# Selective attention and spectral mixing: q and k in runs of 18 tokens, two batches per transfer, on two partition halves

## The chip, the cores and the metric

The kernel runs on one core of a Trainium2 chip. The metric is the device time of one execution in microseconds (us). An execution reads all its inputs from HBM and writes its result there.

## What is computed

Two stages follow each other. The first is causal attention over 8 batches, 8 heads, 576 tokens and 64 dimensions per head, with a bias made of cumulative sums of a selector `s`. The second takes the first 64 Fourier modes along the tokens, mixes their channels with one complex 512x512 matrix per mode, goes back, and adds a projection with a ReLU.

```python
scores = scale * np.matmul(q, k.transpose(0, 1, 3, 2))
cum = np.cumsum(np.maximum(s, 0.0), axis=-1)
bias = -(cum[:, :, :, None] - cum[:, :, None, :])
scores = np.where(causal, -1000000000.0, scores + np.minimum(bias, 0.0))
attn = softmax(scores)
x = np.matmul(attn, v)                      # heads side by side: (8, 576, 512)

X = np.fft.rfft(x, axis=1)[:, :64]
Y[:, :64] = einsum('bmd,mde->bme', X, w_r + 1j * w_i)   # 64 complex 512x512 matrices
u = x + np.fft.irfft(Y, n=576, axis=1)
out = u + np.maximum(u @ w_ch, 0.0)
```

The inputs are float32. The matrices `w_r` and `w_i` are 134 MB of them, and q, k and v 9.4 MB each.

## The kernel before

The attention works on pairs of heads. There are N = 32 steps: step n takes batch n % 8 and the head pair n // 8 (the variable `g`). Each step needs q, k and v of its pair of heads. The weights of the spectral stage are loaded all the time beside this, in tiles of 4 modes x 128 input channels. Once the 8 steps of a head pair `g` are transformed (after step 7, 15, 23 and 31), the products of its 128 channels (`modes`, L444) use the weights, one set of 8 modes per step or so.

**Loads.** All large loads are issued by GpSimd (POOL), in program order, and are cast from float32 to bf16 (or fp16) on the way. `loads_qkv` (L147) makes the list for one step: q, k, and v in two parts. `loads_w` (L200) makes the list of weight transfers, two of 256 KB for each tile, one for each half of the partitions. `load` (L222) mixes the lists it is given evenly and issues them at L226. In step n it mixes the q, k and v of step n + 3 (LA = 3) with the weights that should be on chip by then (`on_chip`). A load into a buffer waits until the last reader of the buffer is done. q and k have LA + 1 = 4 buffers each, v has 5, and the weights have two rings of 11 and 6 tiles beside 8 places in tensors that are not in use yet.

**How q and k lie.** A step's two heads lie on the 128 partitions, 64 partitions to a head, and each partition has R = 9 consecutive tokens of 64 values. A run is therefore 9 x 64 x 4 = 2304 bytes read and 1152 bytes written, and each of q and k is one transfer of 128 runs (144 KB written).

**Transposes.** The scores need the 64 dimensions on the partitions. `transposes(n, which)` (L323) turns q (which = 0) or k (which = 1) with 18 small TensorE transposes (L333) into one PSUM tile, `tr_ps`, of which there is only one buffer. Two copies (L336) take it to SBUF: the first head on partitions 0 to 63 of `qtA` or `ktA`, the second head on partitions 64 to 127 of `qtB` or `ktB`. Row 64 of `qtA` and row 0 of `qtB` hold the negated cumulative sums (`cum_rows`, L315), and the same rows of `ktA` and `ktB` hold ones, so that the matmul adds the bias. The rest of the lower half of `qtB` and `ktB` is zero. The first head's matmuls thus contract over 65 rows, the second head's over 128 (L374).

**The order of one step** (L549 to L573) is written out by hand: loads for step n + 3; `cum_rows(n + 1)`; scores of the first head; `av` (attention times v) of the step before, second head; transposes of q for step n + 1; scores of the second head; transposes of k for step n + 1; the Fourier transform of step n - 1 (`fft`); `av` of the first head; then the modes that are due. TensorE executes this list in order. So a transpose that waits for q or k holds up all that stands behind it on TensorE.

After the steps, the remaining weights of the last group are loaded and multiplied, the result is projected, and 9.4 MB are written out.

Of the kernel before, what the change touches and what calls it, by code (L numbers as in the profile page):

```python
# [11 lines left out]
BF16 = mybir.dt.bfloat16  # L12
# [6 lines left out]
def kernel(  # L19
# [11 lines left out]
    nc = tc.nc  # L31
    B, H, S, D = q.shape
    NM = moe_w_r.shape[0]
    DM = H * D
    P = 128
    NT = (S + P - 1) // P
    tails = [min(P, S - T * P) for T in range(NT)]
    NL = tails[NT - 1]
# [4 lines left out]
    NCH = D + 1  # L43
    N = NG * B
# [4 lines left out]
    WA, WB = 11, 6  # L49
    LA = 3  # L50
    NF = NT - 1
    R = S // (P // 2)
    RP = P // 2
    W = 2 * P
    NWN = S // W
    NK = 2 * NWN
# [1 line left out]
    HP = P // 2  # L58
# [52 lines left out]

    at = ExitStack()
    ap_ = at.enter_context(tc.tile_pool(name="attn", bufs=1))
    qkpool = at.enter_context(tc.tile_pool(name="qk_sb", bufs=LA + 1))
    cumt_sb = ap_.tile([P, NK + 1, NPAIR], FP32, name="cumt_sb")
    cumt4 = ap_.tile([P, NPAIR // 2], FP32, name="cumt4")
    ncum_sb = ap_.tile([NPAIR, S], BF16, name="ncum_sb")
    NQ = 2
    qtA = [ap_.tile([NCH, S], BF16, name=f"qtA{i}") for i in range(NQ)]
    qtB = [ap_.tile([P, S], BF16, name=f"qtB{i}") for i in range(NQ)]  # L120
    ktA = [ap_.tile([NCH, S], BF16, name=f"ktA{i}") for i in range(NQ)]
    ktB = [ap_.tile([P, S], BF16, name=f"ktB{i}") for i in range(NQ)]
    NV = LA + 2
    VW = 66

# [18 lines left out]

    loaded = {}

    def loads_qkv(n):  # L147

        if n >= N:
            return []  # L150
        g, b = divmod(n, B)
        hs = slice(2 * g, 2 * g + 2)
        q2 = qkpool.tile([P, R + 1, D], BF16, name="q2", tag="q2")[:, :R, :]
        k2 = qkpool.tile([P, R + 1, D], BF16, name="k2", tag="k2")[:, :R, :]
        loaded[n] = (q2, k2)
        todo = [
            (dst, src[b, hs].rearrange("h (p r) d -> (h p) r d", r=R))
            for src, dst in ((q, q2), (k, k2))
        ]
        todo += [  # L160
            (
                v2[n % NV][:, : 2 * NWN * W].rearrange("p (w h c) -> p w h c", w=NWN, h=2)[:, :, h, P:],
                v[b, 2 * g + h, : NF * P, :].rearrange("(w p r) d -> p w (r d)", p=P, r=2),
            )
            for h in range(2)
        ]
        return todo

    def loads_tails(g):

        if g >= NG:
            return []
        return [
            (
                v4[g % 2][NL * h : NL * h + NL, :, :D],
                v[:, 2 * g + h, NF * P :, :].rearrange("b t d -> t b d"),
            )
            for h in range(2)
        ]
# [42 lines left out]
    def load(*lists):  # L222

        todo = [((i + 0.5) / len(l), x) for l in lists for i, x in enumerate(l)]
        for _, (dst, src) in sorted(todo, key=lambda t: t[0]):
            nc.gpsimd.dma_start(out=dst, in_=src)  # L226
# [8 lines left out]
    W0 = 3  # L235
    on_chip = []
# [15 lines left out]
    nc.sync.dma_start(out=s_sb, in_=s.rearrange("b h t -> (b h) t"))  # L252
    nc.sync.dma_start(out=ident32, in_=d_ident32)
    nc.sync.dma_start(out=negm32, in_=d_negm)
    first, second, tails0 = loads_qkv(0), loads_qkv(1), loads_tails(0)
    load(first[:2])
    load(loads_w(W0), first[2:] + tails0 + second)
    nc.sync.dma_start(out=Ff_sb, in_=d_Ff.rearrange("(T p) c -> p T c", p=P))
    nc.sync.dma_start(out=ident16h, in_=d_ident16h)
    nc.sync.dma_start(out=G_sb, in_=d_G)  # L260
# [2 lines left out]
    nc.vector.memset(zero, 0.0)  # L263
    nc.scalar.activation(out=zero, in_=zero, func=ACTF.Exp)
    for i in range(NQ):
        nc.vector.memset(qtB[i][0:64, :], 0.0)
        nc.vector.memset(ktB[i][0:64, :], 0.0)
        nc.vector.memset(ktB[i][0:1, :], 1.0)
        nc.vector.memset(ktA[i][D : D + 1, :], 1.0)
    for i in range(NV):  # L270
        for c in (P - 1, W):
            nc.vector.memset(
# [42 lines left out]
    def cum_rows(n):  # L315
        if n >= N:
            return
        g, b = divmod(n, B)
        p0 = b * H + 2 * g
        nc.sync.dma_start(out=qtA[n % NQ][D : D + 1, :], in_=ncum_sb[p0 : p0 + 1, :])  # L320
        nc.sync.dma_start(out=qtB[n % NQ][0:1, :], in_=ncum_sb[p0 + 1 : p0 + 2, :])

    def transposes(n, which):  # L323
        if n >= N:
            return
        src = loaded[n][which]
        dA, dB = ((qtA, qtB), (ktA, ktB))[which]
        g, b = divmod(n, B)
        ps = trpool.tile([P, R, RP], BF16, name="tr_ps", tag="tr")
        for r in range(R):  # L330
            for h in range(2):
                rows = slice(D * h, D * h + D)
                nc.tensor.transpose(ps[rows, r, :], src[rows, r, :], ident16[rows, rows])  # L333
        for dst, rows in ((dA, slice(0, D)), (dB, slice(D, P))):
            copy = (nc.vector.tensor_copy, nc.scalar.copy)[which == 1 and dst is dB]
            copy(  # L336
                out=dst[n % NQ][rows, :].rearrange("d (p r) -> d p r", r=R),
                in_=ps[rows].rearrange("d r p -> d p r"),
            )

    def scores4(n, ps):

        g, b = divmod(n, B)
        i0 = NF * P
        nc.tensor.matmul(
            ps, ident16, negm[:, 2 * W :], start=False, stop=False, skip_group_check=True
        )
        for h, (kt, qt) in enumerate(((ktA, qtA), (ktB, qtB))):
            nc.tensor.matmul(  # L349
                ps[NL * h : NL * h + NL, :], kt[n % NQ][:, i0:], qt[n % NQ][:, i0:],  # L350
                start=False, stop=True, skip_group_check=True,
            )
        nc.scalar.activation(  # L353
            out=p4[n % 2][:, :NL], in_=ps, func=ACTF.Exp,
            bias=cumt4[:, b * (H // 2) + g : b * (H // 2) + g + 1], scale=0.125,
        )

    def scores(n, h):
        g, b = divmod(n, B)
        pidx = b * H + 2 * g + h  # L360
        qt = (qtA, qtB)[h][n % NQ]
        pt = p_sb[(2 * n + h) % NP_]
        keys = (ktA, ktB)[h][n % NQ][:, : NF * P].rearrange("c (w p r) -> c w r p", p=P, r=2)
        for r in range(2):
            ps = scpool.tile([P, 1024], FP32, name="sc_ps", tag="sc")

            for w in range(NWN):
                nc.tensor.matmul(  # L368
                    ps[:, bass.ds(w * S, W)], ident16, negm[:, bass.ts(r, W)],
                    start=True, stop=False, skip_group_check=True,  # L370
                )
            for w, i0, i1 in ((0, 0, 512), (0, 512, S), (1, W, S)):
                c0 = w * S + i0 - w * W
                nc.tensor.matmul(  # L374
                    ps[:, c0 : c0 + i1 - i0], keys[:, w, r, :], qt[:, i0:i1],
                    start=False, stop=True, skip_group_check=True,
                )
            if h == 1 and r == 0:
                scores4(n, ps[:, 2 * S - W : 2 * S - W + NL])
            for w in range(NWN):  # L380
                x = 2 * w + r
                nc.scalar.activation(  # L382
                    out=pt[:, poff[x] : poff[x] + S - w * W], in_=ps[:, w * S : (w + 1) * S - w * W],
                    func=ACTF.Exp, bias=cumt_sb[:, x, pidx : pidx + 1], scale=0.125,
                )
# [155 lines left out]
    with tc.tile_pool(name="sc_psum", bufs=2, space=PSUM) as scpool, \  # L541
            tc.tile_pool(name="tr_psum", bufs=1, space=PSUM) as trpool, \
            tc.tile_pool(name="av_psum", bufs=1, space=PSUM) as avpool:
        cum_rows(0)
        transposes(0, 0)
        transposes(0, 1)
        load(loads_qkv(2))
        pad_p()
        for n in range(N):  # L549
            if n in (0, 2):  # L550
                nc.vector.memset(xs_flat[n // 2].bitcast(FP32), 0.0)
            tails_due = loads_tails(n // B + 1)[n % B - 3 : n % B - 2] if 2 < n % B < 5 else []
            load(loads_qkv(n + LA) + tails_due, loads_w(on_chip[n]))
            cum_rows(n + 1)
            scores(n, 0)
            av(n - 1, 1)
            transposes(n + 1, 0)
            scores(n, 1)
            i = first_pairs[n - N + len(first_pairs)] if n >= N - len(first_pairs) else None
            if i is not None:  # L560
                first_transposed(i, 0)
            transposes(n + 1, 1)
            fft(n - 1)
            av(n, 0)
            if i is not None:
                first_product(i, 0)
                first_transposed(i, 1)
            for c in mode_steps.get(n, []):
                modes(c // NCK, c % NCK)
            if i is not None:  # L570
                first_product(i, 1)
            if n == N // 2:
                nc.gpsimd.dma_start(out=wch_sb, in_=moe_w_ch.rearrange("(dt p) e -> p dt e", p=P))  # L573
        av(N - 1, 1)
        fft(N - 1)
# [354 lines left out]
```

## Time and profile before

| | |
|---|---|
| time, median of 3 runs | 448.7 us (448.08 to 450.4) |
| span of the profiled execution | 445.7 us |
| written by DMA | 93.30 MB, mean 209 GB/s |
| read from HBM | 163.51 MB, 388 GB/s over the span with what is written |
| packets of queue q0 (issued by POOL) | 67984, 81.29 MB |
| q or k transfer, issue to landing | 7.1 us (median of 32 each) |
| weight transfer, issue to landing | 8.0 us |

The page divides the span into 40 slices and gives the busy share of each engine in tenths. Bytes are counted as written: a load that casts float32 to bf16 reads twice what it writes. A group line gives the source line, the engine, the operation, the tile written and the tile read, and how many there are; then the total busy time and the mean of one in ns; then the idle time ahead of them and what ended it. A line of a list of waits names who waited, for what, the sum in us, how often, and the longest. Line numbers are those of the kernel before.

### The profile page before, as it was taken

Reading aid. Unit: us, or ns where it says so; the run is one execution under the profiler, and the core shown is the slowest. Engines: PE = TensorE matmul, PEld = TensorE weight load, DVE = VectorE, ACT = ScalarE, POOL = GpSimd, SP = SyncE. Lnnn points to the kernel's source line nnn. Section 1 sums busy time; section 2 is a strip of 40 time slices with the busy share of each in tenths; the row PEclk is TensorE's granted clock in tenths of the full one; section 3 lists DMA queues with packets and bytes.
Section 4 is the critical chain, followed back from the end, with each engine's and each line's share of the span. In section 5 each row is a group of like instructions: output and inputs, shape, how many; then the busy total and the mean of one; then the engine's idle time right before and its main releaser. Section 6 shows DMA issues by size and latency. Waiting matters only on the chain.

```text
span 445.7 us, 11492 instructions
## 1 busy us (share of the span) xinstructions
PE 355.5 (80%) x4729; PEld 222.3 (50%) x4729; DVE 251.0 (56%) x576; ACT 218.7 (49%) x387; POOL 259.8 (58%) x405
## 2 busy tenths in 40 slices
PE   1889987997575989967767887888897896769994
PEld 1557665665344655644445354556664455433341
DVE  7777764675243656643445445556654454441885
ACT  1586766366242654744426254556550434220593
POOL 7766665755566675556675655566544544430393
PEclk9999997999575889975869796999997999988999
DMA  9999999999999999999999999999999999996598
GB/s 183 201 202 205 204 203 205 204 207 206 208 207 202 196 193 202 208 207 207 205 202 206 206 207 207 207 204 203 207 210 210 209 210 210 209 217 121 173 353 345
DMA packets 77251, 93.30 MB, mean 209 GB/s; under 512 B 30144, under 2 KB 39872, under 8 KB 77200
## 3 DMA queue, kind: packets, MB, share of 16 engines
q0 software_dynamic: 67984, 81.29, 105.5%
q1 hardware_dynamic: 9216, 11.29, 7.8%
q8 instruction: 37, 0.61, 0.5%
q14 instruction: 14, 0.11, 0.1%
HBM read 163.51 MB, written 9.44 MB: 388 GB/s over the span
## 4 chain that ended last, share of the span: by engine, by line
DMA 62%; PE 21%; POOL 5%; issue 5%; DVE 4%; POOLq 1%; ACT 0%; SPq 0%; DVEq 0%
DMA w_sb<-in_moe_w_i_dram 26%; DMA w_sb<-in_moe_w_r_dram 15%; DMA q<-in_q_dram 10%; DMA k<-in_k_dram 9%; PE yp L452 4%; PE sc_ps L374 3%; POOL r_w L766 3%; PE z_ps L624 2%; PE av_ps L403 2%; PE tr_ps L333 2%; PE sc_ps L368 2%; PE ft_ps L429 2%; POOL w_sb L226 2%; DMA qtA<-ncum_sb 1%; DMA xs<-c_negm 1%
## 5 line engine op out<-in xcount | busy, mean ns | idle before, releaser
L382 ACT ACTIVATE p_sb<-sc_ps,cumt_sb 128x576 f16<-128x576 f32 (+1 forms) x256 | 142.0, 636 | 58.7 <-PE sc_ps L374 58.2
L226 POOL DMA_DIRECT2D w_sb<-in_moe_w_r_dram x120 | 71.6, 597 | 61.1 <-DMA w_sb<-in_moe_w_r_dram 18.5
L226 POOL DMA_DIRECT2D w_sb<-in_moe_w_i_dram x120 | 71.3, 595 | 49.4 <-DMA w_sb<-in_moe_w_i_dram 17.3
L226 POOL DMA_DIRECT2D v<-in_v_dram x72 | 51.8, 719 | 22.4 <-DMA w_sb<-in_moe_w_r_dram 7.1
L368 PE MATMUL sc_ps<-negm,ident 128*128 128x256 bf16 x256 | 55.6, 303 | 0.4
L452 PE MATMUL yp<-w_sb,xs 128*32 128x512 bf16 (+1 forms) x480 | 42.5, 431 | 12.3 <-DMA w_sb<-in_moe_w_i_dram 5.6
L403 PE MATMUL av_ps<-v,p_sb 128*128 128x65 f16 x1024 | 45.2, 199 | 0.0
L333 PE MATMUL tr_ps<-ident,q 64*64 64x64 bf16 x576 | 16.6, 205 | 33.3 <-DMA q<-in_q_dram 33.3
L336 DVE COPY ktA<-tr_ps 64x576 bf16<-64x576 bf16 x32 | 24.0, 750 | 33.8 <-PE tr_ps L333 33.8
L403 PEld LDWEIGHTS <-p_sb 128*128 128x128 f16 x1024 | 39.4, 101 | 5.4 <-DVE x_all L413 2.3
L374 PE MATMUL sc_ps<-qtB,ktB 128*128 128x512 bf16 (+2 forms) x192 | 41.4, 330 | 0.0
L336 DVE COPY qtA<-tr_ps 64x576 bf16<-64x576 bf16 x32 | 23.8, 742 | 29.1 <-PE tr_ps L333 28.9
L374 PE MATMUL sc_ps<-qtA,ktA 65*128 65x512 bf16 (+2 forms) x192 | 38.6, 313 | 0.6 <-DMA qtA<-ncum_sb 0.6
L439 DVE CAST xs<-ft_ps 64x128 bf16<-64x128 f32 x128 | 31.4, 284 | 8.3 <-PE ft_ps L429 7.7
L353 ACT ACTIVATE p<-sc_ps,cumt 128x64 f16<-128x64 f32 x32 | 10.1, 314 | 52.7 <-PE sc_ps L349 52.7
L408 DVE TENSOR_REDUCE den<-av_ps 128x5 f32<-128x10 f32 x64 | 10.9, 170 | 43.6 <-PE av_ps L403 42.8
L429 PE MATMUL ft_ps<-Ff_sb,x_all 128*64 128x96 f16 (+1 forms) x640 | 33.2, 224 | 1.0 <-DVE x_all L413 1.0
L452 PEld LDWEIGHTS <-xs 128*32 128x32 bf16 (+1 forms) x512 | 19.8, 145 | 28.4 <-issue 16.6
L413 DVE TENSOR_TENSOR x_all<-av_ps,rcp 128x320 f16<-128x320 f32 x64 | 31.4, 491 | 2.2
L333 PE MATMUL tr_ps<-ident,k 64*64 64x64 bf16 x576 | 16.8, 206 | 19.0 <-DVE qtB L336 10.0
L336 ACT COPY ktB<-tr_ps 64x576 bf16<-64x576 bf16 x32 | 20.3, 634 | 22.3 <-DVE ktA L336 21.4
L333 PEld LDWEIGHTS <-q 64*64 64x64 bf16 x576 | 12.9, 118 | 35.8 <-DMA q<-in_q_dram 34.7
(119 smaller groups left out, 558.1 us busy)
## 6 DMA issues: line engine op xcount, KB each, us to landing
w_sb<-in_moe_w_r_dram POOLq DMA_DIRECT2D x120, 256.0 KB, 8.0
w_sb<-in_moe_w_i_dram POOLq DMA_DIRECT2D x117, 256.0 KB, 8.1
out_dram<-r_w SPq DMA_DIRECT2D x14, 512.0 KB, 3.0
q<-in_q_dram POOLq DMA_DIRECT2D x32, 144.0 KB, 7.1
k<-in_k_dram POOLq DMA_DIRECT2D x32, 144.0 KB, 7.1
v<-in_v_dram POOLq DMA_DIRECT2D x72, 64.0 KB, 6.9
x_all<-in_moe_w_i_dram POOLq DMA_DIRECT2D x6, 256.0 KB, 6.8
out_dram<-r_w SPq DMA_DIRECT2D x6, 256.0 KB, 3.2
```

Source lines behind the costliest of these rows:

```text
L226: nc.gpsimd.dma_start(out=dst, in_=src)
L333: nc.tensor.transpose(ps[rows, r, :], src[rows, r, :], ident16[rows, rows])
L336: copy(out=dst[n % NQ][rows, :].rearrange("d (p r) -> d p r", r=R), in_=ps[rows].rearrange("d r p -> d p r"),)
L368: nc.tensor.matmul(ps[:, bass.ds(w * S, W)], ident16, negm[:, bass.ts(r, W)], start=True, stop=False, skip_group_check=True,)
L374: nc.tensor.matmul(ps[:, c0 : c0 + i1 - i0], keys[:, w, r, :], qt[:, i0:i1], start=False, stop=True, skip_group_check=True,)
L382: nc.scalar.activation(out=pt[:, poff[x] : poff[x] + S - w * W], in_=ps[:, w * S : (w + 1) * S - w * W], func=ACTF.Exp, bias=cumt_sb[:, x, ...
L403: nc.tensor.matmul(ps[:, I, r : r + NCH], lhsT, rhs, start=(i == 0), stop=(i == len(todo) - 1), skip_group_check=True,)
L413: nc.vector.tensor_tensor(out=x_all[:, g, b, :, D * h : D * h + D], in0=ps[:, :, 1 : NCH], in1=rcp.unsqueeze(2).to_broadcast([P, NT, D]), ...
L429: nc.tensor.matmul(ps[HP * h : HP * h + HP, q_, :], x_all[:nT, g, b, T, q_::2], Ff_sb[:nT, T, 3 * HM * h : 3 * HM * (h + 1)], start=(T == ...
L439: nc.vector.tensor_copy(out=xs[g % 2][rows, :, k, h, :, b, :], in_=ps[rows, :, k * HM : (k + 2) * HM].rearrange("p q (r m) -> p q r m", r=2),)
L452: nc.tensor.matmul(ps[32 * cg : 32 * cg + 32, :], cols[k0:, q_, 1 - ri, :, c * MC // 2 + cg], wt[(g, c, ri, cg // 2)][k0:, 2 * (cg % 2) + ...
L766: nc.gpsimd.tensor_tensor(out=rs[i], in0=rs[i], in1=z1s[i], op=ALU.add)
```

## The change

q and k are laid out anew. 32 partitions now hold a head, and each partition holds R = 18 consecutive tokens. A run is 4608 bytes read and 2304 bytes written. q has partitions 0 to 63 and k partitions 64 to 127 of one tile, and the tile has room for two batches. One transfer of q and one of k load both batches; the first two batches are loaded one by one, so that the first can start early. Two such tiles take the place of four buffers each of q and k, and pairs are asked for only in steps of odd n. The transposes of a step are again two calls, but each now takes 9 of the 18 tokens of every partition, of q and of k together. The destinations are `qt` and `kt`, with both heads side by side along the free dimension and 65 rows for either head. The zeros and the 128-row contraction of the second head go away.

The purpose is to move the same bytes of q and k in longer runs and in fewer transfers.

```diff
-    R = S // (P // 2)
-    RP = P // 2
+    RP = P // 4
+    R = S // RP
+    RH = R // 2
...
-    qkpool = at.enter_context(tc.tile_pool(name="qk_sb", bufs=LA + 1))
+    qkpool = at.enter_context(tc.tile_pool(name="qk_sb", bufs=2))
...
-    qtA = [ap_.tile([NCH, S], BF16, name=f"qtA{i}") for i in range(NQ)]
-    qtB = [ap_.tile([P, S], BF16, name=f"qtB{i}") for i in range(NQ)]
-    ktA = [ap_.tile([NCH, S], BF16, name=f"ktA{i}") for i in range(NQ)]
-    ktB = [ap_.tile([P, S], BF16, name=f"ktB{i}") for i in range(NQ)]
+    qt = [ap_.tile([NCH, 2, S], BF16, name=f"qt{i}") for i in range(NQ)]
+    kt = [ap_.tile([NCH, 2, S], BF16, name=f"kt{i}") for i in range(NQ)]
...
-        todo = [
-            (dst, src[b, hs].rearrange("h (p r) d -> (h p) r d", r=R))
-            for src, dst in ((q, q2), (k, k2))
+        t = loaded[n] = loaded[n + 1] = qkpool.tile([P, 2, R * D], BF16, name="qk2", tag="qk2")
+        return [
+            (
+                t[HP * i : HP * i + HP, x0:x1],
+                src[b + x0 : b + x1, hs].rearrange("b h (p r) d -> (h p) b (r d)", r=R),
+            )
+            for x0, x1 in ([(0, 2)] if n else [(0, 1), (1, 2)])
+            for i, src in enumerate((q, k))
         ]
...
-        nc.vector.memset(qtB[i][0:64, :], 0.0)
-        nc.vector.memset(ktB[i][0:64, :], 0.0)
-        nc.vector.memset(ktB[i][0:1, :], 1.0)
-        nc.vector.memset(ktA[i][D : D + 1, :], 1.0)
+        nc.vector.memset(kt[i][D : D + 1], 1.0)
...
-    def transposes(n, which):
+    def transposes(n, half):
...
-        ps = trpool.tile([P, R, RP], BF16, name="tr_ps", tag="tr")
-        for r in range(R):
-            for h in range(2):
-                rows = slice(D * h, D * h + D)
+        src = loaded[n][:, n % 2, :].rearrange("p (r d) -> p r d", d=D)[:, half * RH : half * RH + RH]
+        ps = trpool.tile([P, RH, 2 * RP], BF16, name="tr_ps", tag="tr")
+        for r in range(RH):
+            for i in range(2):
+                rows = slice(HP * i, HP * i + HP)
                 nc.tensor.transpose(ps[rows, r, :], src[rows, r, :], ident16[rows, rows])
-        for dst, rows in ((dA, slice(0, D)), (dB, slice(D, P))):
-            copy = (nc.vector.tensor_copy, nc.scalar.copy)[which == 1 and dst is dB]
+        for i, dst in enumerate((qt, kt)):
+            copy = (nc.vector.tensor_copy, nc.scalar.copy)[half * i]
+            to = dst[n % NQ][:D].rearrange("d h (p r) -> d h p r", r=R)
             copy(
-                out=dst[n % NQ][rows, :].rearrange("d (p r) -> d p r", r=R),
-                in_=ps[rows].rearrange("d r p -> d p r"),
+                out=to[:, :, :, half * RH : half * RH + RH],
+                in_=ps[HP * i : HP * i + HP].rearrange("d r (h p) -> d h p r", h=2),
             )
...
-            load(loads_qkv(n + LA) + tails_due, loads_w(on_chip[n]))
+            load((loads_qk(n + LA) if n % 2 else []) + loads_v(n + LA) + tails_due, loads_w(on_chip[n]))
```

More of the change, by code (lines that the diff above doesn't have):

```diff
@@ L145, with loads_qk @@
     loaded = {}
-    def loads_qkv(n):
+    def loads_qk(n):
         if n >= N:
@@ L152, in loads_qkv, with loads_v @@
         hs = slice(2 * g, 2 * g + 2)
-        q2 = qkpool.tile([P, R + 1, D], BF16, name="q2", tag="q2")[:, :R, :]
-        k2 = qkpool.tile([P, R + 1, D], BF16, name="k2", tag="k2")[:, :R, :]
-        loaded[n] = (q2, k2)
-        todo = [
-            (dst, src[b, hs].rearrange("h (p r) d -> (h p) r d", r=R))
-            for src, dst in ((q, q2), (k, k2))
-        ]
-        todo += [
+        t = loaded[n] = loaded[n + 1] = qkpool.tile([P, 2, R * D], BF16, name="qk2", tag="qk2")
[6 more added lines that the diff above has]
+            for i, src in enumerate((q, k))
+        ]
+    def loads_v(n):
+        if n >= N:
+            return []
+        g, b = divmod(n, B)
+        return [
             (
@@ L166, in loads_qkv @@
         ]
-        return todo
     def loads_tails(g):
@@ L254 @@
     nc.sync.dma_start(out=negm32, in_=d_negm)
-    first, second, tails0 = loads_qkv(0), loads_qkv(1), loads_tails(0)
+    first = loads_qk(0)
     load(first[:2])
-    load(loads_w(W0), first[2:] + tails0 + second)
+    load(loads_w(W0), loads_v(0) + loads_tails(0) + first[2:] + loads_v(1))
     nc.sync.dma_start(out=Ff_sb, in_=d_Ff.rearrange("(T p) c -> p T c", p=P))
@@ L319, in cum_rows @@
         p0 = b * H + 2 * g
-        nc.sync.dma_start(out=qtA[n % NQ][D : D + 1, :], in_=ncum_sb[p0 : p0 + 1, :])
-        nc.sync.dma_start(out=qtB[n % NQ][0:1, :], in_=ncum_sb[p0 + 1 : p0 + 2, :])
-    def transposes(n, which):
+        for h in range(2):
+            nc.sync.dma_start(out=qt[n % NQ][D : D + 1, h, :], in_=ncum_sb[p0 + h : p0 + h + 1, :])
+    def transposes(n, half):
         if n >= N:
             return
-        src = loaded[n][which]
-        dA, dB = ((qtA, qtB), (ktA, ktB))[which]
-        g, b = divmod(n, B)
-        ps = trpool.tile([P, R, RP], BF16, name="tr_ps", tag="tr")
-        for r in range(R):
-            for h in range(2):
-                rows = slice(D * h, D * h + D)
+        src = loaded[n][:, n % 2, :].rearrange("p (r d) -> p r d", d=D)[:, half * RH : half * RH + RH]
[3 more added lines that the diff above has]
+                rows = slice(HP * i, HP * i + HP)
                 nc.tensor.transpose(ps[rows, r, :], src[rows, r, :], ident16[rows, rows])
-        for dst, rows in ((dA, slice(0, D)), (dB, slice(D, P))):
-            copy = (nc.vector.tensor_copy, nc.scalar.copy)[which == 1 and dst is dB]
+        for i, dst in enumerate((qt, kt)):
+            copy = (nc.vector.tensor_copy, nc.scalar.copy)[half * i]
+            to = dst[n % NQ][:D].rearrange("d h (p r) -> d h p r", r=R)
             copy(
-                out=dst[n % NQ][rows, :].rearrange("d (p r) -> d p r", r=R),
-                in_=ps[rows].rearrange("d r p -> d p r"),
+                out=to[:, :, :, half * RH : half * RH + RH],
+                in_=ps[HP * i : HP * i + HP].rearrange("d r (h p) -> d h p r", h=2),
             )
@@ L347, in scores4 @@
         )
-        for h, (kt, qt) in enumerate(((ktA, qtA), (ktB, qtB))):
+        for h in range(2):
             nc.tensor.matmul(
-                ps[NL * h : NL * h + NL, :], kt[n % NQ][:, i0:], qt[n % NQ][:, i0:],
+                ps[NL * h : NL * h + NL, :], kt[n % NQ][:, h, i0:], qt[n % NQ][:, h, i0:],
                 start=False, stop=True, skip_group_check=True,
@@ L360, in scores @@
         pidx = b * H + 2 * g + h
-        qt = (qtA, qtB)[h][n % NQ]
+        qh = qt[n % NQ][:, h, :]
         pt = p_sb[(2 * n + h) % NP_]
-        keys = (ktA, ktB)[h][n % NQ][:, : NF * P].rearrange("c (w p r) -> c w r p", p=P, r=2)
+        keys = kt[n % NQ][:, h, : NF * P].rearrange("c (w p r) -> c w r p", p=P, r=2)
         for r in range(2):
@@ L374, in scores @@
                 nc.tensor.matmul(
-                    ps[:, c0 : c0 + i1 - i0], keys[:, w, r, :], qt[:, i0:i1],
+                    ps[:, c0 : c0 + i1 - i0], keys[:, w, r, :], qh[:, i0:i1],
                     start=False, stop=True, skip_group_check=True,
@@ L546 @@
         transposes(0, 1)
-        load(loads_qkv(2))
+        load(loads_qk(2) + loads_v(2))
         pad_p()
```

## The prediction

> **What bounds the kernel now.** I read the page's engine shares and its slices first, then the chain of waits, then the waits of TensorE, and last the answer by windows.
>
> ```profile
> PE 355.5 (80%) x4729; PEld 222.3 (50%) x4729; DVE 251.0 (56%) x576; ACT 218.7 (49%) x387; POOL 259.8 (58%) x405
> DMA  9999999999999999999999999999999999996598
> q0 software_dynamic: 67984, 81.29, 105.5%
> DMA 62%; PE 21%; POOL 5%; issue 5%; DVE 4%; POOLq 1%; ACT 0%; SPq 0%; DVEq 0%
> ```
>
> No compute engine is above 80%, while the 16 DMA engines stand at 9 tenths in the first 36 slices. The chain that ended last is 62% DMA. The 105.5% of queue q0 is over 100% because packets overlap on an engine.
>
> ```profile
> PE tr_ps L333 <- DMA q<-in_q_dram: 33.3, 12, 6.4
> PE tr_ps L333 <- DVE qtB L336: 10.0, 15, 2.0
> ...
> PE tr_ps L333 <- DMA k<-in_k_dram: 8.4, 8, 2.0
> PE yp L452 <- DMA w_sb<-in_moe_w_i_dram: 5.6, 4, 2.1
> ```
>
> These are TensorE's longest repeated waits (us, times, longest). It waits for q, k and weights to arrive: it runs ahead of the stream and is held by it.
>
> ```profile
> 20.00:320.00 300.00, 245.35 (x3816) 164.22 (x3813) 168.40 (x420) 164.60 (x312) 189.39 (x308) 0.86 1.20 205
> 330.00:390.00 60.00, 49.25 (x455) 28.42 (x452) 30.30 (x55) 19.05 (x27) 27.91 (x48) 0.94 1.12 210
> ```
>
> The last two columns are the DMA share and GB/s written. The attention stage moves 205 GB/s, the stage with weights alone 210. The small difference is what smaller packets cost; it is the whole subject of the change.
>
> Is the stream ever starved? POOL issues 393 transfers, and in the trace 337 of these go out while exactly 7 earlier ones are still under way. The least after 30 us is 4. In quarter-microseconds of the packet records, the number of packets in flight falls below 16 only twice, near 163 us, for 0.06 us of work in all. So to 409 us (landing of the last weight) the time is the sum of the packets' costs, and from there to 445.7 a tail of 36.5 us follows (last modes, results), in which nothing that the change touches runs.
>
> [...] I price it from the trace. With a fixed cost f per data packet and b per byte written, 16 engines x time = packets x f + bytes x b. From 20 to 320 us there are 50,126 data packets and 61.33 MB in 4.80 million engine-ns; from 330 to 390 us 6,109 packets and 12.58 MB in 0.96 million. Solved: **b = 0.0734 ns/B, f = 6.0 ns**. Each written byte is a bf16 half of 2 read bytes, so b is 27.3 GB/s of reads per engine[...]. [...] The weights here are already loaded into halves of 64 partitions and still run at 210 GB/s[...]. [...]
>
> **The change part by part.**
>
> 1. *Longer runs.* q and k are 64 transfers of 128 packets of 1152 B (8,192 in all). After: 4,096 packets of 2304 B, the same bytes. The saving is one fixed cost per merged pair, and its size is the disputed number. Low end: f = 6.0 ns, 4,096 x 6.0 / 16 = 1.5 us. High end: a single 1152 B packet lasts 107 ns and a 2048 B packet 173 ns in the records; that line has an intercept of 22 ns, but packets overlap (share 1.20), so little of the 22 is throughput; taken in full it gives 4,096 x 22 / 16 = 5.6 us. Between: if each size has its own price, a fit over stretches of 2.5 us gives 92 +- 5 ns for 1152 B (stretches of 5 us: 102 +- 7), against 6.0 + 84.6 = 90.6 on the line. A 2304 B packet should cost 6.0 + 169.1 = 175. I take the finer fit: 2 x 92 - 175 = 9 ns, x 4,096 / 16 = **2.3 us**. No run here shows a cast packet of 2304 B.
>
> 2. *Fewer transfers.* 64 become 34 (the first two batches keep single loads). Each ends in 16 completion packets; at f each, 30 x 16 x 6 / 16 = **0.2 us** at most. POOL spends 30 x 0.575 = 17 us less on issuing, but POOL waits for a free place among the transfers anyway; the stream hides it.
>
> 3. *Order of loads and waits.* A pair goes out in the load list of an odd n, where before one batch went. Its tile was last used by the pair before the last, so POOL waits for the second transposes of batch n. In the trace POOL issued q(n+3) 3.1 us (n = 1) and from n = 3 on 6 to 26 us after those transposes had begun. So this wait is over before it is asked; behind it in POOL's queue are v and weights, which would otherwise be held. Nothing.
>
> 4. *Transposes in two halves.* The first half now needs q **and** k. In the trace k landed after TensorE had started on q at nearly every even n from 8 to 28, by 0.2 to 4.3 us (21 us in 9 batches). TensorE will stop longer there; behind it stand the second scores, fft, av and modes. At odd n it has its data a whole iteration early and doesn't stop. TensorE needs 6.8 us per batch where it does not wait (batches 3 to 7), about 8.3 with one set of modes, and the stream gives it 10 to 15. It catches up within the pair. The modes' buffers come free up to some 4 us later every second iteration; 5 transfers in flight x 1.25 us (256 KB at 210 GB/s) cover 6 us. I book nothing, and keep this as the main risk.
>
> 5. *Evictions.* Three DVE copies (739, 760, 750 ns) and one ACT copy (634) per batch, 64x576 each, before and after. The destination now has runs of 9 with steps of 18 elements. Bounds: nothing, to twice as long (2.2 us per batch on DVE). DVE is at 56%; either is under the stream's 10 us per batch. Nothing.
>
> 6. *Second head with 65 rows instead of 128.* The 512-column matmul took 443 ns with 128 rows and 419 with 65; at most 64 x 24 + 64 x 20 + 64 x 9 ns = 3.4 us of TensorE, beside the stream. Memsets (eight become two) run before the constants land at 6.3 us. The two rows of sums per batch stay 64 small transfers. Nothing.
>
> Sum: 2.3 + 0.2 = 2.5 us off the stream; the tail moves with it. 448.7 - 2.4 = **446.3 us** (I leave 0.1 us for dips).
>
> **The rivals.**
>
> *A: the full 22 ns count.* For it: the clean intercept of the durations. Against: the two stages, solved together, leave 6 ns. 5.6 us, and 30 x 22 ns = 0.7 us for completions: 442.4 us.
>
> *B: the longer stop for k starves the stream, and it ends slower.* For it: twelve times TensorE began within 0.05 us of q's landing, so each stop is real, and the weights' buffers are released behind it; at 162, 178 and 245 us only 5 transfers were in flight. Against: the cover of 6 us. If at each of ten even batches 1 us to 0.5 us gets through, that is 5 to 10 us, less the 2.5: some 453 us.
>
> *C: a read of 4608 B is cut in two[...], or is dearer.* The longest cast read here is 4096 B, so nothing in the trace decides it. The packets stay 8,192: 448.5 us.
>
> **How the numbers follow.** Forecast 0.60, A 0.12, B 0.16, C 0.12. The threshold of 0.5% is 446.5 us, almost on the forecast: its case splits, half faster (0.30), half same. Faster: 0.30 + A 0.12 + 0.01 = 0.43. Same: 0.29 + C 0.12 = 0.41. Slower: 0.16. The range runs from 443.2 (most of the way to A) to 449.6 (C, the spread of the runs before, and the mild end of B).
>
> **What would show it.** Packets of 2304 B, 4,096 of them on q0, each about 192 ns long. Queue q0's packets down by some 4,600. The last weight landing near 406.8 instead of 409.2 us, the tail still 36 to 37 us. TensorE waits for k rather than q at L333, in every second batch only. Wrong would be: DMA slices below 9 before 400 us, or POOL idle on TensorE with fewer than 4 transfers in flight (B); packets of 1152 B or of uneven sizes (C); a stream shorter by 5 us (A).

## The result and the profile after

The changed kernel takes **461.48 us** (median of 4 runs, 458.63 to 462.29), the kernel before 448.93 us in the same session. The ratio is 1.0265, 95% interval 1.0212 to 1.0317: slower by 12.6 us, where 2.4 us less was forecast.

The same rows of the page as before, now of the changed kernel: engine shares, the DMA slices, bytes moved in each slice, queue q0, and the shares of the chain.

```profile
PE 382.1 (83%) x4729; PEld 238.6 (52%) x4729; DVE 249.6 (54%) x570; ACT 222.2 (48%) x387; POOL 242.8 (53%) x375
...
DMA  9999999993999999999999999999999999998498
GB/s 180 201 207 206 203 187 204 145 162 50 203 205 210 203 206 207 188 208 207 208 203 203 207 208 202 208 206 207 206 210 209 211 209 210 209 214 157 147 351 347
...
q0 software_dynamic: 63408, 81.29, 101.4%
...
PE 48%; DMA 35%; DVE 6%; POOL 3%; issue 3%; ACT 2%; POOLq 1%; SPq 0%; DVEq 0%; ACTq 0%
```

The packets did what was asked: q0 has 4,576 fewer, 4,096 of data and 480 that end 30 transfers (5,808 packets of 4 B for 363 transfers, 6,288 for 393 before: 16 for each). But the chain, 62% DMA before, is now 48% TensorE and 35% DMA. In slices 8 to 10 of GB/s, each 11.5 us long (80 to 115 us), the stream falls to 145, 162 and 50. It has a hole, and the packet records size it: the engines idle there make up 13.1 us of the whole stream, against 0.06 us before. What follows is shifted, not slowed: 20 MB of queue q0 are written at 120.7 us instead of 105.1, and 80 MB at 414.9 instead of 400.2. The last weight lands at 423.7 us instead of 409.2, and the tail is 36.2 us against 36.5.

Who made the hole? First the lines of POOL's waits (who waited, for what; us in total, times, longest), one of the kernel before and two of the changed one, then POOL's own instructions around the longest one (start, us, what, idle before and its releaser).

```profile
POOL w_sb L226 <- PE yp L452: 6.4, 9, 1.1
```

```profile
POOL w_sb L232 <- PE yp L454: 25.3, 7, 14.4
...
POOL qk L232 <- PE tr_ps L334: 13.3, 3, 7.0
```

```profile
94.37 1.21 POOL L232 DMA_DIRECT2D w_sb<-in_moe_w_r_dram  x2
110.01 0.59 POOL L232 DMA_DIRECT2D w_sb<-in_moe_w_r_dram  x1 [14.44 <-PE yp L454]
```

POOL stood still for 14.4 us because a weight buffer was not free: its reader, the first modes (`yp`), had not run. The transfers already in flight lasted until 102.1 us, so when POOL went on at 110.0 none was left. So TensorE was late. How late it was shows in the view by windows of 30 us; the columns are busy time of PE, PEld, DVE, ACT, POOL, then PEclk, DMA share and GB/s. Before:

```profile
20.00:50.00 30.00, 26.82 (x479) 19.26 (x476) 22.46 (x57) 23.41 (x45) 20.86 (x34) 1.00 1.21 205
50.00:80.00 30.00, 25.76 (x441) 18.26 (x441) 18.52 (x49) 20.55 (x40) 19.96 (x33) 0.89 1.24 204
80.00:110.00 30.00, 27.34 (x466) 18.68 (x463) 20.08 (x53) 17.68 (x34) 18.42 (x31) 1.00 1.19 206
```

After:

```profile
20.00:50.00 30.00, 30.00 (x326) 19.60 (x324) 15.40 (x37) 17.41 (x33) 18.03 (x29) 1.00 1.20 205
50.00:80.00 30.00, 30.00 (x339) 20.05 (x338) 14.57 (x39) 16.25 (x31) 15.10 (x24) 1.00 1.20 197
80.00:110.00 30.00, 30.00 (x333) 18.20 (x335) 13.68 (x36) 13.52 (x25) 10.05 (x16) 1.00 0.73 121
```

TensorE is shown as busy for all of 90 us and yet executes 326 matmuls in the first window where it executed 479. The profile models the ends of matmuls, but their starts say the same: from 20 to 110 us no two are more than 0.6 us apart. TensorE is not waiting; each matmul is longer. One group shows it. The timeline of TensorE: first before, then after, 18 transposes and the 20 matmuls of the Fourier transform.

```profile
46.53 0.47 PE L333 MATMUL tr_ps<-ident,k 64*64 64x64 bf16 x18 [0.54 <-DMA w_sb<-in_moe_w_i_dram]
46.94 0.98 PE L429 MATMUL ft_ps<-Ff_sb,x_all 128*64 128x96 f16 x20
```

```profile
60.30 0.69 PE L334 MATMUL tr_ps<-ident,qk 64*64 64x64 bf16 x18
60.91 1.43 PE L431 MATMUL ft_ps<-Ff_sb,x_all 128*64 128x96 f16 x20
```

Neither group was changed in its work, and both take about 1.46 times as long. The column PEclk says 1.00, but it has no record there: the trace's first clock record of the changed kernel is "full speed" at 111.0 us, and what lies ahead of a first record is shown as full. In the kernel before, the first such record is at 18.4 us. A step takes 10.1 us instead of 6.8 (the transposes of L334 begin at 60.30, 70.38 and 80.47 us), and the first modes start at 103.8 us instead of 80.3.

### The profile page after: what moved, and what is told of

It is laid out like the page before. It is cut to its first block, busy times and chain, and to the rows that moved or that the text cites. A ratio compares the mean times of both kernels' runs of the same rounds, so it can differ in the third digit from the quotient of the medians.

```text
span 459.9 us, 11427 instructions
## 1 busy us (share of the span) xinstructions
PE 382.1 (83%) x4729; PEld 238.6 (52%) x4729; DVE 249.6 (54%) x570; ACT 222.2 (48%) x387; POOL 242.8 (53%) x375
## 4 chain that ended last, share of the span: by engine, by line
PE 48%; DMA 35%; DVE 6%; POOL 3%; issue 3%; ACT 2%; POOLq 1%; SPq 0%; DVEq 0%; ACTq 0%
DMA w_sb<-in_moe_w_i_dram 12%; DMA w_sb<-in_moe_w_r_dram 11%; DMA qk<-in_k_dram 10%; PE sc_ps L376 9%; PE av_ps L405 8%; PE sc_ps L370 6%; PE yp L454 5%; PE ft_ps L431 5%; PE tr_ps L334 5%; PE z_ps L626 3%; POOL r_w L768 3%; PE z_ps L537 1%; DVE kt L338 1%; DVE qt L338 1%; PE xt_ps L616 1%
## 5 line engine op out<-in xcount | busy, mean ns | idle before, releaser
L232 POOL DMA_DIRECT2D w_sb<-in_moe_w_i_dram x120 | 71.3, 597 | 61.2 <-DMA w_sb<-in_moe_w_i_dram 18.2
L376 PE MATMUL sc_ps<-qt,kt 65*128 65x512 bf16 (+2 forms) x384 | 90.2, 352 | 1.2 <-ACT kt L338 1.1
L338 DVE COPY qt<-tr_ps 64x576 bf16<-64x576 bf16 x64 | 47.8, 747 | 65.9 <-PE tr_ps L334 65.9
L334 PE MATMUL tr_ps<-ident,qk 64*64 64x64 bf16 x1152 | 38.2, 217 | 42.1 <-DMA qk<-in_k_dram 19.9
L376 PEld LDWEIGHTS <-kt 65*128 65x128 bf16 x384 | 45.2, 118 | 33.2 <-issue 13.8
L334 PEld LDWEIGHTS <-qk 64*64 64x64 bf16 x1152 | 29.6, 128 | 53.0 <-DMA qk<-in_k_dram 20.6
L405 PE MATMUL av_ps<-v,p_sb 128*128 128x65 f16 x1024 | 52.2, 213 | 0.0
L405 PEld LDWEIGHTS <-p_sb 128*128 128x128 f16 x1024 | 46.5, 110 | 4.7 <-DVE x_all L415 0.5
L338 ACT COPY kt<-tr_ps 64x576 bf16<-64x576 bf16 x32 | 22.9, 716 | 16.4 <-DVE qt L338 15.9
L431 PEld LDWEIGHTS <-x_all 128*64 128x64 f16 (+1 forms) x640 | 25.3, 126 | 10.6 <-DVE x_all L415 1.1
L370 PEld LDWEIGHTS <-ident 128*128 128x128 bf16 x256 | 19.4, 105 | 14.3 <-PE yp L454 5.1
```

Source lines behind the costliest of these rows:

```text
L338: copy(out=to[:, :, :, half * RH : half * RH + RH], in_=ps[HP * i : HP * i + HP].rearrange("d r (h p) -> d h p r", h=2),)
L370: nc.tensor.matmul(ps[:, bass.ds(w * S, W)], ident16, negm[:, bass.ts(r, W)], start=True, stop=False, skip_group_check=True,)
L376: nc.tensor.matmul(ps[:, c0 : c0 + i1 - i0], keys[:, w, r, :], qh[:, i0:i1], start=False, stop=True, skip_group_check=True,)
L405: nc.tensor.matmul(ps[:, I, r : r + NCH], lhsT, rhs, start=(i == 0), stop=(i == len(todo) - 1), skip_group_check=True,)
L431: nc.tensor.matmul(ps[HP * h : HP * h + HP, q_, :], x_all[:nT, g, b, T, q_::2], Ff_sb[:nT, T, 3 * HM * h : 3 * HM * (h + 1)], start=(T == ...
```

## The experiments

**Theory R**: the second head's 128-row matmuls had brought TensorE to its full clock. With 65 rows it stays at half speed until the modes, falls behind, gives buffers back late, and the stream starves. **Theory O**, the prediction's rival B widened: the new order (pairs, two tiles, a half transpose that needs q and k at once) makes the holes.

**128 rows for the second head again.** All else stays as changed.

```diff
+    KR = (NCH, 128)
+    qt = [ap_.tile([P, 2, S], BF16, name=f"qt{i}") for i in range(NQ)]   # kt alike
...
+        nc.vector.memset(kt[i][D:, 1, :], 0.0)   # qt alike
...
-        qh = qt[n % NQ][:, h, :]
+        qh = qt[n % NQ][: KR[h], h, :]   # keys and scores4 alike
```

> The changed kernel, with one part undone: the second head's matmuls contract over 128 rows again (rows 65 to 127 of its qt and kt are zero). Loads, pairs, two tiles and half transposes stay. Theory R (rows: with 65 rows TensorE's clock is granted in full only at 111 us, so that it falls behind and the stream starves for 13 us): full clock near 18 to 20 us, a step of 6.8 us before step 8, no hole in the stream, 446 to 447 us. Theory O (order: the pair's tile wait and the first half's need of q and k together make the holes): holes of POOL near 60, 80 and 95 us stay, 459 to 462 us.

Measured: 447.44 us (20 runs), ratio to before 0.9979, interval 0.9968 to 0.9990. The first full-clock record is at 23.2 us (half again from 36.9, for 6.8 us). Its slices have no hole:

```profile
DMA  9999999999999999999999999999999999996598
GB/s 176 202 206 205 203 207 204 207 203 208 207 209 203 206 204 179 207 206 208 207 202 206 208 208 207 208 207 203 200 210 210 211 211 208 209 218 132 176 352 340
```

TensorE does wait for k in this kernel, as the prediction had feared; here is that line of its waits:

```profile
PE tr_ps L337 <- DMA qk<-in_k_dram: 28.4, 8, 4.9
```

28.4 us in 8 waits, up to 4.9 us each, and the idle DMA adds up to 0.4 us. So the new order makes no hole once TensorE keeps time. R holds.

**The kernel before, with 65 rows for both heads.** The complement: nothing of the loads or the order is changed.

```diff
-    qtA, qtB, ktA, ktB                                # second head on rows 64 to 127
+    qt = [ap_.tile([NCH, 2, S], BF16, name=f"qt{i}") for i in range(NQ)]   # kt alike
...
-                out=dst[n % NQ][rows, :].rearrange("d (p r) -> d p r", r=R),
+                out=dst[n % NQ][:D, h, :].rearrange("d (p r) -> d p r", r=R),
```

> The kernel before, with one part of the change alone: both heads contract over 65 rows, qt and kt as in the changed kernel; loads, buffers and transposes by q and by k as before. Theory R: half clock until the modes of step 8, 10 us per step, TensorE behind by some 25 us at step 8, about 459 to 463 us (a little more or less, as four buffers of q and k forgive more than two pairs: 455 at the least). Theory O: 448 to 449 us.

Measured: 463.37 us, ratio 1.0356 (1.0319 to 1.0392). First full clock at 109.3 us, and, between 20 and 112 us, one wait of 17.6 us of POOL for the modes:

```profile
POOL w_sb L224 <- PE yp L447: 17.6, 1, 17.6
```

This one part of the change alone makes the whole loss. It even ends later than the changed kernel; whether that is for want of the cheaper packets was not tested.

**Three tiles of pairs instead of two.** The edit is `bufs=3` for `qk_sb`.

> The changed kernel with three tiles of pairs of q and k instead of two; 65 rows stay. Theory O: the waits of POOL for the transposes (13.3 us in 3) go and with them most of the loss, 447 to 450 us. Theory R: those waits go, but TensorE at half clock remains, POOL then waits for the modes' buffers instead, 457 to 462 us.

Measured: 462.1 us, ratio 1.0286 (1.0230 to 1.0342). POOL's waits for the transposes go, and the time stays. First POOL's two long waits between 20 and 112 us in the changed kernel, then the one that is left with three tiles:

```profile
POOL w_sb L232 <- PE yp L454: 14.4, 1, 14.4
POOL qk L232 <- PE tr_ps L334: 13.3, 3, 7.0
```

```profile
POOL w_sb L232 <- PE yp L454: 18.6, 1, 18.6
```

The wait for q's and k's tile in the changed kernel was a symptom. Taken away, it leaves a longer wait for the modes, and the idle DMA is no less: 14.3 us ahead of 115 us, against 13.1.

**The clock raised once, at the start.**

```diff
...
+        for _ in range(21):
+            nc.tensor.matmul(wps, wm[:, :P], wm, start=True, stop=True, skip_group_check=True)
         spos = s_sb
```

> The changed kernel with 21 more matmuls of 128x128 by 512 columns on a constant tile at the start, while TensorE waits for the cumulative sums; 65 rows stay. Its time tells whether 65-row steps can hold a full clock that something else has brought: if the clock only has to be raised once, full clock from about 8 us on and 446 to 447 us; if 65-row steps cannot hold it, the clock falls to half within 5 to 10 us after the added matmuls and the time is 459 to 462 us. Theory O: 459 to 462 us at either clock.

Measured: four runs of 445.9, 453.1, 459.4 and 463.0 us. So spread a result has no meaningful median, and I use its trace (of the run of 459.35 us). It has clock records from the start: full at 5.8 us, half at 12.7 (the added matmuls end at 8.3), full again only at 98.0. With records there, the page shows the half clock as it is (0.50 from 20 to 80 us), and the matmuls at it are the length that those of the changed kernel had. The clock's slices, then the transposes from 20 to 50 us here and in the changed kernel (ns, min/median/max):

```profile
PEclk9555555579997579975659976958999799999999
```

```profile
L339 PE MATMUL tr_ps<-ident,qk x110: 237/238/259, 21.0 to 50.0; 64*64 64x64 bf16 x110
```

```profile
L334 PE MATMUL tr_ps<-ident,qk x108: 237/238/259, 21.2 to 47.2; 64*64 64x64 bf16 x108
```

In the kernel before the median over the same stretch is 193 ns. So the changed kernel was at half clock before its first record. And 65-row steps don't surely hold a full clock that something else has brought. TensorE paused for 1.4 and 2.1 us around 9 and 12 us of that run, so the fall need not be due to the rows alone. Whether the clock held in the run of 445.9 us, no trace shows.

**Work added, rows left at 65.** If it is activity that counts, it need not come from the score matmuls.

```diff
             ps = scpool.tile([P, 1024], FP32, name="sc_ps", tag="sc")
+            if h == 1 and n < B:
+                nc.tensor.matmul(
+                    ps[:, :512], ident16, negm[:, :512], start=True, stop=True, skip_group_check=True
+                )
```

> The changed kernel, 65 rows and all, with work added: in steps 0 to 7 each of the two score tiles of the second head gets one more matmul of 128 rows by 512 columns, whose result the next matmul overwrites (16 more matmuls, 0.22 us each at full clock). If TensorE's activity is what sets its clock, the added work makes the kernel faster: clock full by some 25 us, 446 to 448 us. If rows of the score matmuls matter in some other way, or the stream is held by something else, 462 us and a little more.

Measured: 447.74 us (20 runs), ratio 0.9992 (0.9974 to 1.0011); first full clock at 24.1 us. Sixteen superfluous matmuls in 4,745 take some 13 us off: the changed kernel is 12.6 us slower than before, this one 0.8 faster, each against its own session.

**128 rows in the first 8 steps alone.** `KR[h * (n < B)]` in place of `KR[h]`.

> The changed kernel with 128 rows for the second head in steps 0 to 7 alone, 65 rows from step 8 on. If the loss comes only from the stretch ahead of the first modes, where attention alone has to raise the clock, 447 to 448 us as with 128 rows throughout. If the later stretches lose too, between 448 and 461 us, with holes in the stream after 110 us.

Measured: 448.25 us, ratio 0.9993 (0.9973 to 1.0013). The loss arises ahead of the first modes. After them the rows make no difference that these runs can tell.

**96 and 97 rows.** As the first experiment, with another number in `KR`.

> The changed kernel with 96 rows for the second head (rows 65 to 95 zero). If what keeps the clock at half is counted in strips of 32 rows, 65 and 96 rows are the same three strips: half clock until the modes, 459 to 463 us. If it is counted in rows, 96 is half way between 65 (461.5 us) and 128 (447.4 us), and the clock comes late or not surely: anything between, or a spread from run to run.

> The changed kernel with 97 rows for the second head (rows 65 to 96 zero). If strips of 32 rows count, 97 rows take four strips like 128: full clock near 20 us, 447 to 448 us. If rows count, it is like 96 rows, whatever that gives.

Measured with 96: twelve runs from 446.6 to 462.2 us, six below 449.0 and six from 454.7 on; the profiled one, at 447.85 us, reached full clock at 47.7 us. With 97: 447.34 us (446.26 to 450.98), ratio 0.9988 (0.9970 to 1.0007); the profiled one, the slowest of twelve, has full clock first at 23.2 us, then half from 36.8 to 84.6 and 2.7 us of idle DMA. Strips of 32 rows alone don't explain it: 96 rows are not like 65, which lost in every run of the changed kernel. Rows alone would make 96 and 97 alike, and they are not, though twelve runs of each leave room. That question stays open.

**Both heads with 128 rows.**

> The changed kernel with 128 rows (zeros from row 65 on) in the score matmuls of both heads. Theory R: clock full by 16 to 23 us and no early fall back to half (with 128 rows for the second head alone it fell once, at 36.9 us for 6.8 us); the stream was whole in that run but for 0.4 us, so at most 0.5 us less than there: 446.5 to 447.5 us. Rival (rows cost time or power): slower than with the second head alone.

Measured: 446.85 us (22 runs), ratio 0.9972 (0.9961 to 0.9983). Full clock from 19.4 us, ahead of the modes with one fall, of 3.4 us at 36.4; no hole at all. It is the fastest version here, 1.3 us (0.8 to 1.7) faster than the kernel before, but its interval overlaps that of 128 rows for the second head.

**Short packets again.** The kernel with 128 rows for the second head, loaded in short packets and one batch per transfer.

```diff
-        t = ... qkpool.tile([P, 2, R * D], BF16, name="qk2", tag="qk2")
+        t = ... qkpool.tile([P, 2, 2, RH * D + 64], BF16, name="qk2", tag="qk2")
...
-                t[HP * i : HP * i + HP, x0:x1],
-                src[b + x0 : b + x1, hs].rearrange("b h (p r) d -> (h p) b (r d)", r=R),
+                t[HP * i : HP * i + HP, x, :, : RH * D],
+                src[b + x, hs].rearrange("h (p y r) d -> (h p) y (r d)", y=2, r=RH),
```

> The kernel of 128 rows for the second head, with q and k in the new layout but loaded as before: one batch per transfer, and each run of 18 tokens cut into two of 9 with a gap in the destination, so 64 transfers and 8192 packets of 1152 B. Against the same kernel with long runs (447.4 us) this is the price of the packets alone. By the prediction's sum 2.5 us more (449.9); by the fixed cost of 6.0 ns alone 1.7 us more (449.1); by the difference that the kernel of 128 rows showed to before 0.9 us more (448.4).

Measured: 448.94 us, ratio 1.0027 (1.0007 to 1.0047). Against 0.9979 with long runs that is 0.0048, or 2.2 us, give or take 1.0 by the two intervals (1.6 us by the medians). The prediction's 2.5 fits, and so does 1.7; the smallest of the three, 0.9, lies just outside. The packets are not quite alone in this: a pair's first batch can also land earlier, and TensorE waits 12.2 us for k instead of 28.4. And the traces show no shorter stream: the last weight lands at 408.8 us with long runs and at 408.9 with short ones, but these two runs took 447.16 and 447.08 us, so they can't tell.

**All versions side by side.** Their traces order themselves by one time, that at which the first modes begin. At 79.4 to 81.7 us (before, and every version with 128 rows or added work) and at 85.0 (96 rows) the DMA engines idle at most 0.02 us ahead of 115 us. At 93.7 us (97 rows) they idle 2.6 us, at 101.9 (clock raised once) 8.8, and at 103.2 to 103.8 (the changed kernel, 65 rows in the kernel before, three tiles) 13.1 to 14.3.

## Why the prediction was wrong

**Step 6 failed**: "Second head with 65 rows instead of 128 ... Nothing". It priced the rows by the length of a matmul, 443 against 419 ns, and booked at most 3.4 us of TensorE off the path. Those two figures are means over both clocks. At one clock the lengths are alike: at full clock the 512-column matmul takes 379 ns with 128 rows and 380.5 with 65 (medians of the kernel before), and at half clock 634 with either. What the step left out is that with these rows, or with other work in their place, TensorE got another clock in the first 8 steps: full at 18.4 us before (with one fall of 6.8 us ahead of the modes), at 111.0 us after, at 23.2 us with the rows put back and at 24.1 us with the work added. In the kernel before the rise falls into the first 128-row score matmuls:

```profile
17.60 0.93 PE L374 MATMUL sc_ps<-qtB,ktB 128*128 128x512 bf16 x3
18.87 0.54 PE L374 MATMUL sc_ps<-qtB,ktB 128*128 128x512 bf16 x3
```

With 128 rows put back into the changed kernel it came later, 5 us after the first of them (18.2 and 23.2 us). The step's cost is not zero but 13 to 15 us: the changed kernel is 12.6 us slower than before and the one with 128 rows 1.0 us faster, and in the kernel before, 65 rows cost 463.37 less 448.42, or 15.0.

**Step 4** had a premise that fell with it. "TensorE needs 6.8 us per batch" was read from a stretch at full clock and carried over. At half clock it is 10.1 us; over 8 steps that is 8 x 3.3 = 26 us of delay, and the modes were 23.5 us late. The cover of some 6 us of transfers in flight was right in size (from POOL's last issue, done at 95.6 us, to the last landing at 102.1) and no match for that. What the step called its main risk, the longer stop for k, is real (28.4 us in 8 waits) and costs at most 0.4 us of stream.

**Rival B** named the outcome, slower through a starved stream, but the wrong cause. It expected ten small leaks at the even batches; there was one large hole ahead of the first modes (10.2 us of idle engines), with two smaller ones before it (2.2 and 0.4).

**Steps 1 and 2** stood as far as the packets go. There are 4,096 packets of 2304 B on q0, 192 ns each as forecast, so rival C is out: no run of 4608 B was cut. Their worth, from the comparison with short packets, is 2.2 +- 1.0 us against 2.5, and rival A's 6.3 us is out. Yet the kernel with 128 rows for the second head gains only 0.9 us on before (0.4 to 1.4), and its last weight lands at 408.8 us, not at 406.8. The rest of the change costs about 1.2 us then, which is what the short-packet version shows against before (0.3 to 2.1). Where it goes was not settled.

**Step 3** held where TensorE kept time: with 128 rows POOL has no wait for q's and k's tile, where the changed kernel has 13.3 us. **Step 5** held too: the DVE copies stayed at 749 and 762 ns, the ACT copy rose from 634 to 714 ns, and of TensorE's matmuls only the first scores waited for it, for 1.1 us.

Being busy was not enough for the full clock: in the changed kernel TensorE was busy without a gap from 20 to 110 us and stayed at half, by the lengths of its matmuls (a transpose took 237 ns, where it took 193 in the kernel before). What was executed counted too, not only that something was.

## What to carry to other kernels

Before you book smaller matmuls as free, ask what they do to TensorE's clock, above all in a stretch where the clock has yet to rise: in the kernel before, 65 rows in place of 128 alone moved the first full-clock record from 18.4 to 109.3 us. Look for that record, and compare the length of a group of instructions that the change leaves alone (18 transposes: 0.47 and 0.69 us). A part that is not the bound can become it: the stream here stayed whole as long as the first modes began by 85 us, and TensorE, which had slack for that at 6.8 us per step, had none at 10.1. When a wait is taken away and the time stays, as with the third tile, it was a symptom.

## What was not expected of the hardware

- TensorE, busy all of the time, stayed at half clock for 90 us with 65 rows in all score matmuls of q and k; with 128 rows in those of one head it rose at 18 to 23 us, and with 96 rows it rose at 47.7 us in the one run that was traced, while the times of twelve fell into two halves, below 449.0 and from 454.7 us on. The rows added to the changed kernel hold zeros, so it is not the values in them. Sixteen extra matmuls of 128 rows by 512 columns had the same effect (24.1 us). What exactly decides it was not shown.
- Half clock made these small matmuls longer by 1.46, not by 2 (18 transposes 0.69 against 0.47 us, 20 Fourier matmuls 1.43 against 0.98).
- A cast packet of 2304 B written from 4608 B read lasts 192 ns, on the line that 1152 B (107 ns) and 2048 B (173 ns) give.
